# Side matmuls in the last key tiles of an attention loop, and a PSUM bank that returns to the scores three half tiles later

## The chip, the core and the metric

The kernel runs on one NeuronCore of a Trainium2 chip. The core has a matrix engine (TensorE, "PE" in the profile, with its weight loads as "PEld"), VectorE ("DVE"), ScalarE ("ACT"), GpSimd ("POOL") and SyncE ("SP", which here issues the DMAs). Each engine takes its instructions in order and waits for the others by semaphores. Matrix products go to PSUM, eight banks of 128 x 512 float32; VectorE and ScalarE empty them. The metric is the device time of one execution in microseconds (us).

## What is computed

One transformer block with adaptive layer norm on 2048 tokens of width 512: multi-query attention with 32 heads of 16 (one key and value head), then a bilinear gated feed-forward network of inner width 1792.

```python
mod = (silu(c) @ w_mod).reshape(1, 6, 1, 512)      # sa, ca, ga, sb, cb, gb
h = layernorm(x) * (1 + ca) + sa
q, k, v = h @ wq (32 heads), h @ wk, h @ wv        # k, v: 2048 x 16
p = softmax(q k^T / 4);  o = p v
x = x + ga * (o @ wo)
h = layernorm(x) * (1 + cb) + sb
x = x + gb * (((h @ w_gate) * (h @ w_up)) @ w_down)
```

All products whose precision matters are made from two float16 halves of each operand, as three terms (high x high, low x high, high x low). One 128 x 512 result over 512 inputs takes 4 x 3 = 12 matmuls, and one of the down projection, over 1792 inputs, takes 14 x 3 = 42.

## The kernel before

**Units and steps.** The attention runs in 32 units (`NU`): 4 blocks of 512 queries, and in each block 8 groups of 4 heads. A unit goes over 16 key tiles of 128 keys (`KT`), each in two half tiles, so it has 32 steps (`NSTEP`) and the loop has 1024. In a step stand, in this order: half of the row-maximum work (`max_half(0)`: a score matmul into a bank "mx" at L507 and a max reduction on VectorE at L509), two score matmuls with their exps on ScalarE (`qk_exp`, L549 and L551), and the other half of the maximum work. The maximum work is 40 steps (`LEAD`) ahead of the rest, so the last 40 steps of the loop have none. On odd steps follow the four products P times V of the key tile before (`pv`, L558, two passes each). On even steps side work may follow.

**Banks.** Scores use two banks "sc" in turn, and every third score the bank "spare", if `spare["scores"]` is set. Maxima use three banks "mx"; "pv" and "misc" are one bank each. A score matmul waits until the exp of the last score in its bank is done.

**Side work.** While the loop is in block b, PE also does the rest of block b-1: the output projection `wo_work` (4 groups of 12 matmuls), four transposes with the second layer norm (`ln2_work`), gate and up (28 groups of 12) and down (4 groups of 42). Groups are taken by two, as a `duo`: each matmul is cut into two of 64 rows, one of each group, that run side by side on the two halves of the array. One such couple is a "pair". A duo of groups of n matmuls has two turns of n pairs; in the second the halves are swapped. It holds the banks "misc" and "spare". When it ends, its first group is emptied at once (`g0.post`) and the second (`g1.post`) two steps later, from `late`. While a duo runs, or one waits whose gate is open, or `spare["held"]` is over zero, the scores keep to their two banks.

**The planner.** The queue `fill` is filled at step 16 of a block's first unit (L1120 to L1128). Each entry has a step by which it is due. On every even step `pace` works out how many pairs must go per even step so that all are done in time, and adds this to `credit` (9 at most); for the last batch, with its due step past 992, `RESERVE / PAIR` pairs are left out of the count and so kept for the tail. `fill_gap` then issues a burst of at most 6 pairs (`BURST`): it divides what is left of the turn by the credit, rounds that to a number of bursts, and issues one of them. A burst ends with its turn. A duo begins only if `open_gate` allows it and, in the last 16 steps (`2 * LAST_TILES`), not at all.

**The tail.** After the loop come the last P times V and `pv_out` (L564 to L572: ScalarE copies the sums out, SyncE writes them and the row sums to their places). What `fill` still holds becomes `tail`, in plain form: full-height matmuls (L465). The last normalisation goes through DMAs: row sums are read back (`rc`, L579), inverted on VectorE (L582, L583), written, and read spread over partitions (`rr`, L587), then multiplied and split (L591 to L595). `cover(budget)` issues matmuls of `tail`, counted at 216 ns, between these steps, so that PE has work while they run. Then `wo_work(3)`, `ln2_work(3)`, the rest of `tail`, and `ffn_work(3)` follow; nothing of attention is left to run beside them. The last step of a down group is L746 on VectorE and an output DMA on SyncE (L748); that of a wo group is L640, and that of an up group L731.

Of the kernel before, what the change touches and what calls it, by code (L numbers as in the profile page):

```python
# [21 lines left out]
NB = 4  # L22
BT = S // NB
UB = H // 4
NU = NB * UB
# [8 lines left out]
FILL0 = 18  # L34
QPRE = 20
QPRE0 = 26
RESERVE = 35000.0
NRM_GAP = 2
BN_GAP = 1
LN_GAP = 2  # L40
# [2 lines left out]
BURST = 6  # L43
NHF = 10
V_STEP = 34
DUE = 12
QDUE = 40
LAST_TILES = 8
PAIR = 218.0


# [1 line left out]
def adaln_mqa_glu_kernel(ctx: ExitStack, tc: tile.TileContext, x_in, wq_in, wk_in, wv_in, wo_in,  # L53
# [384 lines left out]
    def half(p, g, i, r, start, stop):  # L438
        left, right = g.op(i)
        nc.tensor.matmul(p, left[64 * r:64 * r + 64], right[64 * r:64 * r + 64], start=start, stop=stop)  # L440

    def duo(g0, g1, tags=("misc", "spare")):

        ps = g0.pre(tag=tags[0]), g1.pre(tag=tags[1])
        n = g0.n
        for turn in range(2):
            for i in range(n):
                for r in range(2):
                    half(ps[r ^ turn], (g0, g1)[r ^ turn], i, r, turn == 0 and i == 0, turn == 1 and i == n - 1)
                if turn == 0 or i < n - 1:  # L450
                    yield i == n - 1
        g0.post(ps[0])

        def late():
            spare["held"] -= 1
            g1.post(ps[1])

        spare["held"] += 1
        after(2, late)
# [84 lines left out]
    def qk_exp(u, kt, p, a):  # L544
        s = sst[u % 3]
        if (u, kt, p) not in ptl:
            ptl[u, kt, p] = work.tile([128, 2, D], F32, name="P", tag="P", bufs=4)
        t = ps_sc()
        nc.tensor.matmul(t, kst[64 * a:64 * a + 50, kt * 128:(kt + 1) * 128],  # L549
                         s[64 * a:64 * a + 50, p, :], start=True, stop=True)  # L550
        nc.scalar.activation(ptl[u, kt, p][:, a, :], t, AF.Exp)  # L551

    def pv(u, kt):
        if kt == 0:
            pvb[u] = psum.tile([128, 512], F32, name="pv", tag="pv", bufs=1)
        for j in range(4):
            p, a = divmod(j, 2)
            nc.tensor.matmul(pvb[u][32 * j:32 * j + 32, :], vst[:, kt, :], ptl[u, kt, p][:, a, :],  # L558
                             start=(kt == 0), stop=(kt == KT - 1))

    def pv_out(u):
        b, g = divmod(u, UB)
        ev = work.tile([128, BT], F32, name="ev", tag="ev", bufs=3)
        nc.scalar.activation(ev, pvb[u], AF.Copy)  # L564
        if g % 2 == 0:
            oc[b, g // 2] = work.tile([128, BT], F32, name="oc", tag="oc", bufs=2)
            rsum[b, g // 2] = dram.tile([8, BT], F32, name=f"rs{b}_{g // 2}")
        h = 4 * (g % 2)
        for j in range(4):
            r = 16 * (h + j)  # L570
            nc.sync.dma_start(oc[b, g // 2][r:r + 16, :], ev[32 * j:32 * j + 16, :])
        nc.sync.dma_start(rsum[b, g // 2][h:h + 4, :], ev[16:128:32, :])  # L572
# [30 lines left out]
    def after(delay, f):  # L603
        if tick[0] is None:
            f()
        else:
            timers.setdefault(tick[0] + delay, []).append(f)
# [329 lines left out]
    NSTEP = 32  # L937
# [3 lines left out]
    def drain_posts():  # L941
        todo = posts[:]
        posts.clear()
        if tick[0] is not None:
            tick[0] += 1
            todo += timers.pop(tick[0], [])
        for f in todo:
            f()

    def max_half(a):  # L950
        u, i = divmod(mstep[0], NSTEP)
        if a == 1:
            mstep[0] += 1
        if u >= NU:
            return
        max_mm(u, i, a)
        if a == 1 and u + 1 < NU and i == (QPRE if u else QPRE0):
            load_q(u + 1)
        if i == NSTEP - 1 and a == 1:
            max_fin(u)  # L960
            (_, f, g), = max_rows(u)
            later[mstep[0] + 2] = (f, g)
# [9 lines left out]
    fill = deque()  # L972
    cur = {"gen": None, "left": 0, "swapped": -9}
    credit = [0.0]

    def pace(step):
# [4 lines left out]
        for _, kind, what, due in fill:  # L981
            n += 4.0 if kind == "solo" else 2 * what[0].n
            kept = RESERVE / PAIR if due > (NB * UB - 1) * NSTEP else 0.0
            most = max(most, (n - kept) / max((due - step) / 2, 1.0))
        return most

    def open_gate(step):
        if not fill:
            return False
        gate = fill[0][0]  # L990
        if gate[0] is None:
            gate[0] = step + gate[1]
        return gate[0] <= step

    def fill_gap(step):


        if cur["gen"] is None:
            if not open_gate(step):
                return  # L1000
            _, kind, what, due = fill.popleft()
            if kind == "solo":
                _, f, post = what
                credit[0] -= 4.0
                f()
                if post:
                    posts.append(post)
                return
            if NU * NSTEP - step < 2 * LAST_TILES:
                fill.appendleft(([0, 0], kind, what, due))  # L1010
                return
            begin(step, what, due)
        parts = max(1, round(cur["turn"] / max(credit[0], 1.0)))
        burst(step, min(-(-cur["turn"] // parts), BURST))

    def begin(step, two, due, tags=("misc", "spare")):
        cur.update(gen=duo(*two, tags=tags), left=2 * two[0].n, turn=two[0].n, second=False, due=due, swapped=-9)

    def burst(step, n):
        for _ in range(n):  # L1020
            swap = next(cur["gen"], None)
            credit[0] -= 1.0
            cur["left"] -= 1
            cur["turn"] -= 1
            if swap is None:
                cur["gen"], cur["left"] = None, 0
                return
            if swap:
                cur["turn"], cur["second"], cur["swapped"] = cur["left"], True, step
                return  # L1030
# [57 lines left out]
    for u in range(NU):  # L1088
        b, g = divmod(u, UB)
        if u == 1:  # L1090
            side.extend(dlist)
        for i in range(NSTEP):
            step = u * NSTEP + i
            kt, p = divmod(i, 2)
            drain_posts()
            spare["scores"] = not spare["held"] and cur["gen"] is None and not (fill and fill[0][1] == "duo" and open_gate(step))
            max_half(0)
            qk_exp(u, kt, p, 1)
            qk_exp(u, kt, p, 0)
            max_half(1)  # L1100
            if p == 1:
                if kt == 0:
                    if u > 0:
                        pv(u - 1, KT - 1)
                        posts.append(lambda u=u: pv_out(u - 1))
                else:
                    pv(u, kt - 1)
                late_max()
            elif fill or cur["gen"]:
                credit[0] = min(credit[0] + pace(step), 9.0)  # L1110
                if credit[0] >= 1.0:
                    fill_gap(step)
            side_step(step)
            if u > 0 and g % 2 == 0 and i in (4, 8, 14):
                if i == 4:
                    nrm = normalise((u - 1) // UB, ((u - 1) % UB) // 2)
                nrm[(4, 8, 14).index(i)]()
            if i == 16 and u > 0 and g == 0:
                ln = ln2_work(b - 1)
                due = (b + 1) * UB * NSTEP + (DUE if b < NB - 1 else -8)  # L1120
                gate = [step + 4, 0]
                for two in twos(wo_work(b - 1)):
                    fill.append((gate, "duo", two, due))
                for gap, it in zip((TR_GAP, LN_GAP, LN_GAP, LN_GAP), ln):
                    fill.append(([None, gap], "solo", it, due))
                gate = [None, FFN_GAP]
                for two in ffn_twos(b - 1):
                    fill.append((gate, "duo", two, due))  # L1128
# [7 lines left out]

    u = NU - 1

    if cur["gen"] is not None:
        assert cur["second"]  # L1140
        for _ in cur["gen"]:
            pass
    pv(u, KT - 1)
    pv_out(u)
    ring["tags"] = [("misc", 1), ("spare", 1)] + [("mx", NMX)] * NMX + [("sc", NSC)] * NSC
    tail = deque(plain(g) for _, _, two, _ in fill for g in two)

    def cover(budget):
        while tail and budget > 0:
            drain_posts()  # L1150
            if next(tail[0], None) is None:
                tail.popleft()
            budget -= 216
        drain_posts()
# [3 lines left out]
            for _ in plain(g):  # L1158
                pass

    cover(6000)
    nrm = normalise(NB - 1, KC - 1)
    nrm[0]()
    cover(3000)
# [31 lines left out]
```

## Time and profile before

| | us |
|---|---|
| runs (3): median, lowest, highest | 1826.44, 1825.76, 1830.4 |
| profiled execution, its own time | 1827.18 |
| span of that execution, first to last instruction | 1825.4 |
| first tail matmul behind the last P times V | 1661.82 |
| busy in the span: PE, VectorE, ScalarE, GpSimd | 1714.7, 1438.3, 1217.3, 488.7 |

Times in the rows of a profile count from the start of the span. A row of the timeline has the start, the duration of the merged instructions, the engine, the line, the operation, output and inputs, and the number of instructions; in brackets stands how long the engine was idle before it and what ended this. A matmul of 64 rows is recorded by itself, so a pair is two records; one P times V has two records for each of its four matmuls. "Granted clock" is the share of its full clock that TensorE had.

### The profile page before, as it was taken

How to read it: one execution, taken by the hardware profiler on the slowest of the kernel's cores; microseconds unless marked ns; L12 is line 12 of the kernel's file. 1: busy time of each engine (PE TensorE's matmuls, PEld its weight loads, DVE VectorE, ACT ScalarE, POOL GpSimd, SP SyncE). 2: the span in 40 equal slices, each digit the busy share in tenths (PEclk: the TensorE clock that was granted, in tenths of full speed). 3: DMA queues.
4: the chain of work that ended last, by engine and by line, in shares of the span. 5: the costliest groups of instructions: out<-in, count | busy, mean ns of one | idle time of the engine just before them, and what ended most of it. 6: DMA issues, size and time to landing. Idle time of an engine off the chain costs nothing.

```text
span 1825.4 us, 32237 instructions
## 1 busy us (share of the span) xinstructions
PE 1714.7 (94%) x12643; PEld 554.1 (30%) x12643; DVE 1438.3 (79%) x2441; ACT 1217.3 (67%) x2269; POOL 488.7 (27%) x688
## 2 busy tenths in 40 slices
PE   6899999889989999999999999999989999998999
PEld 3332222222223333333223333333223323322444
DVE  7877999999998888888998888888989888911210
ACT  4567788777777767776677767676777777772110
POOL 5834453436566811010021010100011010111130
PEclk9999999999999999999999999999999999998999
DMA  5212222112221200000100000000100000001000
GB/s 189 91 69 94 60 69 61 49 44 65 82 70 55 55 15 9 5 14 17 50 9 15 9 15 9 6 14 20 46 8 15 9 15 9 11 4 39 18 1 23
DMA packets 49795, 66.58 MB, mean 36 GB/s; under 512 B 16166, under 2 KB 30314, under 8 KB 49644
## 3 DMA queue, kind: packets, MB, share of 16 engines
q1 hardware_dynamic: 48060, 64.33, 11.4%
q8 instruction: 99, 1.62, 0.4%
q14 instruction: 52, 0.43, 0.1%
q10 hardware_dynamic: 1584, 0.20, 0.1%
HBM read 51.12 MB, written 8.92 MB: 33 GB/s over the span
## 4 chain that ended last, share of the span: by engine, by line
PE 68%; DVE 17%; ACT 10%; issue 2%; DMA 2%; POOL 1%; SPq 0%; DVEq 0%; POOLq 0%; ACTq 0%
PE pv L558 22%; PE misc L440 17%; DVE mpart L509 13%; PE mx L507 10%; PE sc L549 10%; PE misc L465 8%; ACT P L551 8%; DVE gf L731 1%; DMA xbig<-in_A_x_dram 1%; ACT ev L564 1%; DVE x L640 0%; DVE x L746 0%; ACT qf L476 0%; DVE oc L591 0%; ACT q L475 0%
## 5 line engine op out<-in xcount | busy, mean ns | idle before, releaser
L509 DVE TENSOR_REDUCE mpart<-mx 128x1 f32<-128x512 f32 x2048 | 1294.2, 684 | 172.3 <-PE sc L549 136.3
L551 ACT ACTIVATE P<-sc 128x512 f32<-128x512 f32 x2048 | 1097.7, 599 | 391.6 <-PE sc L549 385.0
L549 PE MATMUL sc<-sst,kst 50*128 50x512 f16 x2048 | 630.5, 382 | 52.7 <-ACT P L551 35.3
L507 PE MATMUL mx<-kst,sst 48*128 48x512 f16 x2048 | 656.3, 383 | 22.8 <-DVE mpart L509 19.6
L558 PE MATMUL pv<-P,vst 128*32 128x512 f32 x4096 | 552.2, 612 | 0.0
L507 PEld LDWEIGHTS <-sst 48*128 48x128 f16 x2048 | 161.8, 94 | 602.7 <-issue 545.7
L732 POOL TENSOR_SCALAR glu<-gf 128x512 f16<-128x512 f32 x56 | 34.6, 618 | 556.0 <-DVE gf L731 555.9
L549 PEld LDWEIGHTS <-kst 50*128 50x128 f16 x2048 | 136.5, 94 | 107.0 <-issue 66.8
L440 PE MATMUL misc<-h2T,wg 64*128 64x512 f16 x1008 | 134.6, 375 | 7.7 <-DVE gf L731 7.7
L558 PEld LDWEIGHTS pv<-P,vst 128*32 128x32 f32 x4096 | 81.1, 108 | 186.4 <-issue 181.7
L440 PE MATMUL misc<-h2T,wu 64*128 64x512 f16 x1008 | 132.6, 375 | 0.4 <-ACT g L725 0.4
L731 DVE TENSOR_TENSOR gf<-misc,g 128x512 f32<-128x512 f32 x56 | 38.3, 686 | 102.4 <-PE misc L465 62.9
L594 POOL TENSOR_SCALAR och<-oc 128x512 f16<-128x512 f32 x15 | 9.3, 618 | 305.4 <-DVE oc L591 165.9
L440 PE MATMUL misc<-wd,glu 64*128 64x512 f16 x672 | 85.6, 375 | 1.9 <-DVE x L746 1.1
L725 ACT ACTIVATE g<-misc 128x512 f32<-128x512 f32 x56 | 34.0, 608 | 78.7 <-PE misc L465 75.5
L465 PE MATMUL misc<-wd,glu 128*128 128x512 f16 x336 | 74.0, 382 | 0.0
L440 PEld LDWEIGHTS <-wg 64*128 64x128 f16 x1008 | 50.7, 94 | 71.8 <-issue 19.4
L440 PEld LDWEIGHTS <-wu 64*128 64x128 f16 x1008 | 50.3, 94 | 60.2 <-issue 8.8
L733 POOL TENSOR_TENSOR glu<-gf,glu 128x512 f16<-128x512 f32 x56 | 64.7, 1155 | 4.7
L440 PE MATMUL misc<-h,wq 64*128 64x512 f16 x384 | 52.9, 391 | 1.6 <-ACT qf L476 1.6
L815 POOL TENSOR_TENSOR wsl<-wsl 128x448 f32<-128x448 f32 (+1 forms) x40 | 39.0, 975 | 55.9 <-DMA wsl<-in_B_w_up_dram 30.3
L817 POOL TENSOR_TENSOR kwb<-kwb,wsl 128x448 f32<-128x448 f32 (+1 forms) x40 | 47.6, 1189 | 3.1
(214 smaller groups left out, 912.8 us busy)
## 6 DMA issues: line engine op xcount, KB each, us to landing
wsl<-in_B_w_gate_dram SPq DMA_DIRECT2D x32, 224.0 KB
wsl<-in_B_w_up_dram SPq DMA_DIRECT2D x32, 224.0 KB
wsl<-in_B_w_down_dram SPq DMA_DIRECT2D x28, 256.0 KB
sst<-qd SPq DMA_DIRECT2D x186, 32.0 KB
qd<-q SPq DMA_DIRECT2D x16, 256.0 KB
oc<-ev SPq DMA_DIRECT2D x128, 32.0 KB
rr<-ri SPq DMA_DIRECT2D x16, 256.0 KB
xl<-in_A_x_dram SPq DMA_DIRECT2D x16, 256.0 KB
```

The costliest lines, as they stand in the source:

```text
L440: nc.tensor.matmul(p, left[64 * r:64 * r + 64], right[64 * r:64 * r + 64], start=start, stop=stop)
L465: nc.tensor.matmul(p, left, right, start=i == 0, stop=i == g.n - 1)
L507: nc.tensor.matmul(m, s[64 * a:64 * a + 48, p, t * 128:(t + 1) * 128], kst[64 * a:64 * a + 48, kc * 512:(kc + 1) * 512], start=True, stop= ...
L509: nc.vector.tensor_reduce(mparts[u][:, a, p, t, kc:kc + 1], m, axis=AX.X, op=OP.max)
L549: nc.tensor.matmul(t, kst[64 * a:64 * a + 50, kt * 128:(kt + 1) * 128], s[64 * a:64 * a + 50, p, :], start=True, stop=True)
L551: nc.scalar.activation(ptl[u, kt, p][:, a, :], t, AF.Exp)
L558: nc.tensor.matmul(pvb[u][32 * j:32 * j + 32, :], vst[:, kt, :], ptl[u, kt, p][:, a, :], start=(kt == 0), stop=(kt == KT - 1))
L731: nc.vector.tensor_tensor(gf, p, st["g", f], op=OP.mult)
L732: nc.gpsimd.tensor_scalar(st["glu"][:, 0, f, :], gf, 1.0, 0.0, op0=OP.mult, op1=OP.add)
L733: nc.gpsimd.tensor_tensor(st["glu"][:, 1, f, :], gf, st["glu"][:, 0, f, :], op=OP.subtract)
L815: nc.gpsimd.tensor_tensor(acc if i == 0 else t, t, t, op=OP.mult)
L817: nc.gpsimd.tensor_tensor(acc, acc, t, op=OP.add)
```

## The change

Four things are edited. `late` still empties the second bank two steps after the duo, but the count that keeps the scores off that bank is lowered three steps later, by `free`. The rule of the last 16 steps is gone; instead `open_gate` refuses a duo of groups of n matmuls when fewer than 2 * ceil(n/6) + 2 steps are left: 6 for n = 12, 16 for n = 42. In a first turn `fill_gap` takes at least as many pairs as are needed to end that turn two steps before the loop does. A duo that is still in its second turn when the loop ends is finished behind the last P times V and `pv_out`, and its pairs (216 ns each) count towards the first `cover`. For the last batch the reserve falls from 35000 to 31000 ns and the due step moves from 1016 to 1020.

```diff
-RESERVE = 35000.0
+RESERVE = 31000.0
...
-LAST_TILES = 8
+LAST_DUE = -4
...
         def late():
+            g1.post(ps[1])
+            after(3, free)
+
+        def free():
             spare["held"] -= 1
-            g1.post(ps[1])
...
     def open_gate(step):
         if not fill:
             return False
+        if fill[0][1] == "duo" and NU * NSTEP - step < 2 * -(-fill[0][2][0].n // BURST) + 2:
+            return False
...
-            if NU * NSTEP - step < 2 * LAST_TILES:
-                fill.appendleft(([0, 0], kind, what, due))
-                return
             begin(step, what, due)
         parts = max(1, round(cur["turn"] / max(credit[0], 1.0)))
-        burst(step, min(-(-cur["turn"] // parts), BURST))
+        n = min(-(-cur["turn"] // parts), BURST)
+        if not cur["second"]:
+            n = max(n, -(-cur["turn"] // max((NU * NSTEP - 2 - step) // 2, 1)))
+        burst(step, n)
...
-                due = (b + 1) * UB * NSTEP + (DUE if b < NB - 1 else -8)
+                due = (b + 1) * UB * NSTEP + (DUE if b < NB - 1 else LAST_DUE)
...
-    if cur["gen"] is not None:
-        assert cur["second"]
-        for _ in cur["gen"]:
-            pass
     pv(u, KT - 1)
     pv_out(u)
+    left = cur["left"]
+    if cur["gen"] is not None:
+        assert cur["second"] and NU * NSTEP - cur["swapped"] > 2
+        for _ in cur["gen"]:
+            drain_posts()
...
-    cover(6000)
+    cover(6000 - 216 * left)
```

## The prediction, made before the changed kernel was timed

> **What bounds the kernel now.** I read the page first, for the engines and the groups of instructions.
>
> ```profile
> span 1825.4 us, 32237 instructions
> PE 1714.7 (94%) x12643; PEld 554.1 (30%) x12643; DVE 1438.3 (79%) x2441; ACT 1217.3 (67%) x2269; POOL 488.7 (27%) x688
> L465 PE MATMUL misc<-wd,glu 128*128 128x512 f16 x336 | 74.0, 382 | 0.0
> ```
>
> TensorE bounds most of the span, but not evenly, so the place matters. The last row tells what stands behind the loop: 336 full-height matmuls of the down projection are 8 groups of 42, four of the last block and four of block 2. So the whole down projection of block 2 (168 matmuls) is left for the tail. Next I read the windows of 5 us around the end of the loop. Columns: stretch, its length, busy time (and instructions) of PE, PEld, DVE, ACT, POOL, then granted clock, DMA share, GB/s.
>
> ```profile
> 1635.00:1640.00 5.00, 4.82 (x36) 1.38 (x36) 0.88 (x2) 4.02 (x8) 0.10 (x1) 1.00 0.01 3
> 1640.00:1645.00 5.00, 3.41 (x23) 0.56 (x16) 0.41 (x1) 3.59 (x8) 3.42 (x4) 1.00 0.00 0
> ...
> 1655.00:1660.00 5.00, 4.32 (x24) 0.67 (x20) 0.00 (x0) 2.17 (x4) 0.00 (x0) 0.50 0.00 0
> ```
>
> From 1640 no engine is full, and by 1655 the granted clock is 0.50. The timeline of that stretch shows why nothing is full. It has one key tile (two steps of the loop) per block; L549 are the scores, L440 side pairs, L558 P times V.
>
> ```profile
> 1637.72 0.39 PE L549 MATMUL sc<-sst,kst 50*128 50x512 f16 x2
> ...
> 1637.95 1.03 PE L440 MATMUL misc<-h2T,wu 64*128 64x512 f16 x8
> ...
> 1640.58 0.39 PE L549 MATMUL sc<-sst,kst 50*128 50x512 f16 x2
> ...
> 1641.66 0.86 PE L549 MATMUL sc<-sst,kst 50*128 50x512 f16 x2 [0.68 <-ACT P L551]
> ...
> 1643.44 0.39 PE L549 MATMUL sc<-sst,kst 50*128 50x512 f16 x2
> ```
>
> A key tile with four side pairs (1637.72 to 1640.58) takes 2.86 us, and one with none (1640.58 to 1643.44) also 2.86. The scores have two banks, and the second pair of scores waits for the exp that empties them (0.68 us). Side pairs fit into that wait for nothing. After 1639 there are none, because the old kernel begins no side duo in the last 16 steps; six key tiles run with the gap open, and then at a reduced clock.
>
> **The change part by part.** A step is half a key tile; 1024 steps, side bursts on even ones.
>
> *How many pairs move.* At step 784 the planner queues 2 wo duos of 24 pairs, 14 gate/up duos of 24, 2 down duos of 84, and 4 transposes counted as 4: 568 units. Before it keeps back 35000/218 = 160.6 and aims at step 1016: 407.4 over 115 even steps from 786, or 3.54 a burst. The 400 units ahead of the down duos then end with the 113th burst, step 1010. The trace agrees: its last burst of four pairs is at 1637.95. After, it keeps 31000/218 = 142.2 and aims at 1020: 425.8/117 = 3.64, so the 400 are done with the 110th burst, at step 1004. At 1006 a down duo may open (18 steps left, 2*7+2 = 16 needed). Its first turn of 42 pairs must run in 7 bursts of 6 (1006 to 1018), and the second turn puts 6 into 1020 and 1022. That makes **54 pairs in the loop**, 30 behind the last P times V, and 84 matmuls in the tail in place of 168.
>
> *The tail.* A pair of half-height matmuls or one full one costs the PE the same:
>
> ```profile
> 1600.14 1.46 PE L440 MATMUL misc<-h2T,wu 64*128 64x512 f16 x12
> ```
> ```profile
> 1696.70 124.77 PE misc L465 x578
> ```
>
> 124.77/578 = 0.216 us a matmul; the 12 halves are six pairs, 1.46 us with the last one's drain. The tail is one stream of matmuls, so 54 fewer are 54 x 0.216 = **-11.7 us**. What the removal could uncover is the last normalisation, for which this work is the cover. PE, DVE and SyncE there:
>
> ```profile
> 1658.25 3.64 PE L558 MATMUL pv<-P,vst 128*32 128x512 f32 x16
> 1661.82 15.24 PE L465 MATMUL misc<-wd,glu 128*128 128x512 f16 x66
> ...
> 1679.81 0.39 PE L465 MATMUL misc<-wo,och 128*128 128x512 f16 x1 [0.80 <-DVE och L594]
> 1680.53 8.38 PE L465 MATMUL misc<-wo,och 128*128 128x512 f16 x38 [0.34 <-DVE och L595]
> ```
> ```profile
> 1671.92 0.75 DVE L746 SCALAR_TENSOR_TENSOR x<-misc,sca,x 128x512 f32<-128x512 f32 x1 [31.51 <-PE misc L465]
> 1672.59 0.23 DVE L582 TENSOR_SCALAR rc<-rc,kb 128x32 f32<-128x32 f32 x1
> ```
> ```profile
> 1665.66 0.53 SPq L572 DMA_DIRECT2D rs<-ev  x1
> 1667.36 0.32 SPq L579 DMA_DIRECT2D rc<-rs  x1
> ```
>
> Before, 66 matmuls cover it and PE still waits 0.80 + 0.34 us. After, 30 pairs and 38 matmuls cover it, 68, nearly the same. On the chain, two things move. The reciprocal (L582) stood behind L746, which waited for the first down group (42 matmuls); now both L746 of the duo come after 30 pairs, about 1661.8 + 6.6, and end by +8.2. But the duo's first output DMA is now issued ahead of the rc read on SP, so that read goes from +5.5 to about +7.9, lands an estimated 1.5 to 2 us later (the rs write, issued by 1666.2, let rc go 1.2 us on), and L582 starts near +9.7 instead of +10.8. PE comes to wo sooner too, since its clock stays up. I take -0.3 us; bounds are -1.1 (the wait gone) and +2.1 (no gain on the DVE side and the read's 2.4 us all on the chain). Behind wo, 28 matmuls stay ahead of the transposes as before, and 18 (3.9 us) behind them instead of 74; the last h2T half is needed only 9 matmuls further on, so that still holds.
>
> *The clock.* Two P times V take 3.64 us at that reduced clock. A key tile with six pairs, behind the max work, at full clock:
>
> ```profile
> 1599.91 0.39 PE L549 MATMUL sc<-sst,kst 50*128 50x512 f16 x2
> ...
> 1601.77 1.06 PE L558 MATMUL pv<-P,vst 128*32 128x512 f32 x8
> ...
> 1602.81 0.55 PE L549 MATMUL sc<-sst,kst 50*128 50x512 f16 x2
> ```
>
> Its P times V, from 1601.77 to the next score, takes 1.04, so two are 2.0 to 2.1: **-1.6 us**. The 66 matmuls take 15.24 where 66 x 0.216 and 0.17 of drain are 14.4: **-0.8 us**. [...]
>
> *The last nine key tiles, with six pairs each.* Before:
>
> ```profile
> 1631.01 1.07 PE L558 MATMUL pv<-P,vst 128*32 128x512 f32 x8
> ...
> 1651.03 1.06 PE L558 MATMUL pv<-P,vst 128*32 128x512 f32 x8
> ...
> 1654.10 1.93 PE L558 MATMUL pv<-P,vst 128*32 128x512 f32 x8
> ```
>
> From 1631.01 to the last block's start at 1658.25 they take 27.2 us. The tile of six pairs above takes 2.90 (1599.91 to 1602.81). Nine are 26.1; I add 0.2 because the first must wait for the last up group's VectorE product in the spare bank: 26.3, **-1.0 us**. The dear end is six pairs beside the max work:
>
> ```profile
> 1556.87 1.06 PE L558 MATMUL pv<-P,vst 128*32 128x512 f32 x8
> 1560.13 1.07 PE L558 MATMUL pv<-P,vst 128*32 128x512 f32 x8
> 1563.05 1.07 PE L558 MATMUL pv<-P,vst 128*32 128x512 f32 x8
> ```
>
> The first interval holds six pairs and is 3.26, the second three and is 2.92. Nine at 3.26 would be 29.3, +2.1. I take the tile without max work, since none runs in the last 40 steps.
>
> *Steps 786 to 1004.* Followed burst by burst, the faster pace changes little: 15 bursts of six before and after, 4 of five against 5, but two of the sixes come earlier, beside the max work, where six cost 0.34 more than three (3.26 and 2.92): +0.7. The stretch without it has two fewer; I take 0.2 for each, between 0.34 and the nothing of 2.90 against 2.86: -0.4. **+0.3 us.**
>
> *The spare bank.* Only where no further duo waits do scores take the bank back: six times, at steps 40, 296, 524, 552, 780 and 814. There the score matmul stands before the evacuation:
>
> ```profile
>   DVE x L640: 3.9, 3
>   ACT qf L476: 1.9, 2
>   DVE x L746: 1.3, 2
> ```
> ```profile
> 926.32 0.39 PE L507 MATMUL mx<-kst,sst 48*128 48x512 f16 x1
> 928.48 0.39 PE L549 MATMUL sc<-sst,kst 50*128 50x512 f16 x2 [1.77 <-DVE x L640]
> ...
> 930.41 1.93 PE L558 MATMUL pv<-P,vst 128*32 128x512 f32 x8
> ```
> ```profile
> 174.30 1.06 PE L558 MATMUL pv<-P,vst 128*32 128x512 f32 x8
> ...
> 176.78 1.06 PE L558 MATMUL pv<-P,vst 128*32 128x512 f32 x8
> ```
>
> At best all of it goes: -7.1 us. At worst nothing goes, and three half tiles each run at two banks' 2.86 a key tile instead of three banks' 2.48 (174.30 to 176.78): 18 x 0.19 = +3.4. Most of the wait is not the bound, though: VectorE works through it without a break, on the same evacuation and the max reductions, and stands idle only behind it:
>
> ```profile
> 932.92 1.29 DVE L509 TENSOR_REDUCE mpart<-mx 128x1 f32<-128x512 f32 x2 [1.25 <-PE sc L549]
> ```
> ```profile
> 1345.47 1.89 DVE L509 TENSOR_REDUCE mpart<-mx 128x1 f32<-128x512 f32 x3 [0.51 <-PE sc L549]
> ```
>
> I count these two idle times as won, 1.8 us, and give back 0.8: 0.57 (3 x 0.19) at step 40, where no VectorE evacuation hides the two banks, and 0.2 for the five others. **-1.0 us.**
>
> *Sum.* -11.7 - 1.6 - 0.8 - 0.3 - 1.0 + 0.3 - 1.0 = -16.1. The profiled execution took 1827.18 us (its span 1825.4 and 1.8 around it): 1811.1. It stands 0.7 above the runs' median 1826.44. I say **1811**.
>
> **The rivals.**
> 1. *The clock still falls.* [...] Then the 1.6 and 0.8 stay, and 1.5 of the last two key tiles (1651.03 to 1654.10 and to 1658.25: 3.07 and 4.15 us in place of 2.86): 1811 + 3.9 = 1815. For it: a short stop (the wait of 1.77 us is followed by a P times V of 1.93). Against it: with side pairs the clock reads 1.00 to 1640. 12%.
> 2. *The normalisation is uncovered*, because the output DMA goes ahead of the rc read: +2.4, and with six pairs a tile at the dear price (+2.1 in place of -1.0) another 3.1: 1813 to 1817. The rows of SP speak for the first, the timeline at 1599.91 against the second. 12%.
> 3. *The stalls at the spare bank were all real*: -7.1 instead of -1.0, 1805. VectorE's unbroken row speaks against it. 8%.
> 4. *It does not do what it says*: the gate/up pairs end one burst or two later than I count; from step 1010 the down duo stays shut, and the last tiles run empty as now, 1826. The margin is one even step (1008 would still open). 4%.
> 5. *Slower.* Scores held to two banks behind every duo and not behind six: 56 duos end in the loop, at 0.57 us each 31.9, so 1811 + 1.0 + 31.9 = 1844. It decides from 27 ends on (15.1/0.57). Against it: between duos of one queue the scores are shut out already, and the key tiles there show no third bank. 3%.
>
> The forecast itself has 61%.
>
> **How the numbers follow.** The range joins the forecast with its neighbours: below, the spare bank's -7.1 (1805); above, the clock rival with some of the second (1815 to 1819): 1804 to 1819. Outside lie rivals 4 and 5 and the tails, under 2 in 10. A measurement of this kernel tells about 0.3% (5.5 us) from no change: faster needs less than 1821. Forecast, rivals 1 to 3 and a little doubt: faster 0.91, same 0.06, slower 0.03.
>
> **What would show it.** In the windows: PE near 4.8 of 5 and clock 1.00 from 1635 to the tail. In the groups: L465 misc<-wd,glu x252 instead of x336, and L440 misc<-wd,glu x840 instead of x672. In the timeline: twelve L440 rows in each of the last nine key tiles at 2.9 us. In the waits: no PE sc L549 <- DVE x L640. If key tiles of six pairs take 3.27 there, or wo waits over 2 us for och, or the clock drops all the same, the term of that name was wrong.

## The result and the profile after

The changed kernel takes 1812.04 us (median of 6 runs, 1807.56 to 1813.56) where the kernel before takes 1826.10 (6 runs). The ratio is 0.9916, with a 95% interval of 0.9904 to 0.9928: 14 us, or 0.8%, less. The forecast was 1811. The profiled execution took 1810.53 us, with a span of 1808.8, which is 16.6 below the span before.

First the groups of instructions of the changed kernel (lines have moved by three; L440 is the side pair, L468 the full-height matmul):

```profile
span 1808.8 us, 32406 instructions
PE 1706.7 (94%) x12727; PEld 557.4 (31%) x12727; DVE 1434.5 (79%) x2441; ACT 1218.1 (67%) x2269; POOL 490.5 (27%) x688
L440 PE MATMUL misc<-wd,glu 64*128 64x512 f16 x840 | 106.4, 375 | 1.9 <-DVE x L749 1.1
L468 PE MATMUL misc<-wd,glu 128*128 128x512 f16 x252 | 55.1, 379 | 0.0
```

One down duo has gone from full height (336 to 252) to pairs (672 to 840 halves), as counted. Next the windows at the end of the loop; the columns are those of the windows shown before.

```profile
1640.00:1645.00 5.00, 5.00 (x48) 2.89 (x48) 0.00 (x0) 3.45 (x8) 0.00 (x0) 1.00 0.00 0
...
1655.00:1660.00 5.00, 5.00 (x44) 2.17 (x42) 0.00 (x0) 2.77 (x5) 0.00 (x0) 1.00 0.00 0
1660.00:1665.00 5.00, 5.00 (x48) 2.24 (x46) 0.00 (x0) 0.00 (x0) 0.00 (x0) 1.00 0.13 31
```

PE is busy in all of them, and the granted clock stays at 1.00, where it was 0.50 from 1655 before. PE's timeline from the ninth last key tile on:

```profile
1630.05 1.07 PE L561 MATMUL pv<-P,vst 128*32 128x512 f32 x8
...
1653.69 1.07 PE L561 MATMUL pv<-P,vst 128*32 128x512 f32 x8
1654.69 0.50 PE L552 MATMUL sc<-sst,kst 50*128 50x512 f16 x2
1654.91 1.57 PE L440 MATMUL misc<-wd,glu 64*128 64x512 f16 x12
1656.21 0.50 PE L552 MATMUL sc<-sst,kst 50*128 50x512 f16 x2
1656.63 2.18 PE L561 MATMUL pv<-P,vst 128*32 128x512 f32 x16
1658.75 6.65 PE L440 MATMUL misc<-wd,glu 64*128 64x512 f16 x60
1665.33 8.38 PE L468 MATMUL misc<-wd,glu 128*128 128x512 f16 x38
1673.54 10.84 PE L468 MATMUL misc<-wo,och 128*128 128x512 f16 x48
```

Six pairs (12 records) stand in the key tile, which takes 2.94 us (1653.69 to 1656.63); nine of them take 26.6 (1630.05 to 1656.63) where the nine before took 27.2 with 12 pairs in all. The two last P times V take 2.18 instead of 3.64. Behind them come 30 pairs, then 38 matmuls, and the 48 of wo run through: of the waits of 0.80 and 0.34 us for `och`, 0.14 us is left in this execution. On the chain that they cover:

```profile
1665.44 1.41 DVE L749 SCALAR_TENSOR_TENSOR x<-misc,sca,x 128x512 f32<-128x512 f32 x2 [34.14 <-PE misc L440]
1668.47 0.24 DVE L585 TENSOR_SCALAR rc<-rc,kb 128x32 f32<-128x32 f32 x1 [1.63 <-DMA rc<-rs]
```
```profile
1666.22 0.34 SPq L751 DMA_DIRECT2D out_dram<-x  x1
1666.67 0.37 SPq L582 DMA_DIRECT2D rc<-rs  x1
```

The output DMA does go ahead of the read of the row sums, and VectorE now waits for that read (1.63 us). It still starts 9.7 us behind the last P times V (1668.47 - 1658.75), not 10.8.

Last, what the scores waited for, with the total in us and the number of times:

```profile
  ACT P L554: 31.4, 115
  ACT qf L479: 0.6, 1
```

The waits for L640 and L746 (5.2 us in five) have gone.

Where the 16.6 us went, by stretches. Each number is the difference of the starts of the P times V rows just ahead of two steps (spans up to the first and from the last):

| stretch (steps) | before | after | |
|---|---|---|---|
| up to 38 | 167.53 | 168.51 | +1.0 |
| 38 to 50, bank returns at 40 | 16.65 | 19.63 | +3.0 |
| 50 to 294 | 331.72 | 330.24 | -1.5 |
| 294 to 304, returns at 296 | 16.35 | 15.84 | -0.5 |
| 550 to 562, returns at 552 | 20.31 | 18.59 | -1.7 |
| 776 to 788, returns at 780 | 17.70 | 17.15 | -0.6 |
| 788 to 1006 | 332.41 | 331.75 | -0.7 |
| 1006 to the last but one P times V | 27.24 | 26.58 | -0.7 |
| from there to the end | 167.15 | 152.17 | -15.0 |

The stretches between that are left out agree to 0.03 us. No bank returns in the rows "up to 38" and "50 to 294"; over the thirteen profiles of this case they scatter from 165.7 to 170.8 and from 328.7 to 332.0, so their +1.0 and -1.5 are not put down to the change.

### The profile page after: what moved, and what is told of

It reads as the page before. It is cut to its first block, busy times and chain, and to the rows that moved or that the text cites. A ratio compares the mean times of both kernels' runs of the same rounds, so it can differ in the third digit from the quotient of the medians.

```text
span 1808.8 us, 32406 instructions
## 1 busy us (share of the span) xinstructions
PE 1706.7 (94%) x12727; PEld 557.4 (31%) x12727; DVE 1434.5 (79%) x2441; ACT 1218.1 (67%) x2269; POOL 490.5 (27%) x688
## 4 chain that ended last, share of the span: by engine, by line
PE 69%; DVE 15%; ACT 11%; issue 2%; DMA 2%; POOL 1%; SPq 0%; DVEq 0%; ACTq 0%; POOLq 0%
PE pv L561 22%; PE misc L440 18%; DVE mpart L512 12%; PE mx L510 10%; PE sc L552 10%; ACT P L554 8%; PE misc L468 7%; DVE gf L734 1%; ACT ev L567 1%; DMA xbig<-in_A_x_dram 1%; DVE x L643 0%; DMA wsl<-in_B_w_gate_dram 0%; DVE mh L522 0%; ACT qf L479 0%; ACT q L478 0%
## 5 line engine op out<-in xcount | busy, mean ns | idle before, releaser
L440 PE MATMUL misc<-h2T,wg 64*128 64x512 f16 x1008 | 133.9, 375 | 7.7 <-DVE gf L734 7.7
L440 PE MATMUL misc<-h2T,wu 64*128 64x512 f16 x1008 | 132.3, 375 | 0.5 <-ACT g L728 0.5
L440 PE MATMUL misc<-wd,glu 64*128 64x512 f16 x840 | 106.4, 375 | 1.9 <-DVE x L749 1.1
L440 PEld LDWEIGHTS <-wg 64*128 64x128 f16 x1008 | 50.5, 94 | 71.4 <-issue 18.3
L440 PEld LDWEIGHTS <-wu 64*128 64x128 f16 x1008 | 50.1, 94 | 60.4 <-issue 8.2
L440 PEld LDWEIGHTS <-glu 64*128 64x128 f16 x840 | 46.1, 94 | 46.5 <-issue 5.7
L468 PE MATMUL misc<-wd,glu 128*128 128x512 f16 x252 | 55.1, 379 | 0.0
L440 PE MATMUL misc<-h,wq 64*128 64x512 f16 x384 | 53.0, 392 | 1.6 <-ACT qf L479 1.6
```

The costliest lines, as they stand in the source:

```text
L468: nc.tensor.matmul(p, left, right, start=i == 0, stop=i == g.n - 1)
```

## The experiments

**The two parts apart.** First the later return alone, in the kernel before; then the rest without it.

```diff
         def late():
-            spare["held"] -= 1
             g1.post(ps[1])
+            after(3, free)
+
+        def free():
+            spare["held"] -= 1
```

> The kernel before with the later return of the second bank alone. Theory (the wait at the spare bank counts only where VectorE idles behind it): 1 us less than before, within 0.3% of it; in the profile the waits of scores for L640 and L746 are gone, the key tiles at steps 552, 780 and 814 are shorter by 0.5 to 1.7 us each and those at step 40 longer by 1 to 3. Rival (the stalls were all real): 6 to 7 us less. Rival (two banks cost the whole difference, nothing is won): 3.4 us more.

Measured: 1828.68 us, ratio 1.0004 (0.9992 to 1.0017). By itself the later return gives nothing that can be measured. In its profile the return at 552 takes 18.58 us for 550 to 562 (20.31 before), and the one at 780 17.16 (17.70), as expected; 38 to 50 takes 18.59 instead of 16.65. 810 to 838, around the return at 814, takes 44.41 instead of 43.60, which is against the expectation; the granted clock is 0.50 there from 1341.1 to 1348.0. The interval (1.5 us less to 3.1 more) leaves out the rival of 6 to 7 us less and, just, that of 3.4 more. The theory's 1 us less lies inside it.

The changed kernel with the old `late`:

```diff
         def late():
-            g1.post(ps[1])
-            after(3, free)
-
-        def free():
             spare["held"] -= 1
+            g1.post(ps[1])
```

> The changed kernel with the second bank returned at once, as before. Theory: it keeps 15.1 of the 16.1 us, so about 15 us less than the kernel before (ratio 0.992), with 54 pairs fewer behind the loop and the clock at 1.00 there. If the later return carried the gain instead, it would stay within 3 us of the kernel before.

Measured: 1812.99 us, ratio 0.9924 (0.9912 to 0.9937). The work at the end of the loop carries the gain. The changed kernel lies 0.8 thousandths lower (0.9916), within the intervals of both.

**The clock without the pairs.** The kernel before, with unread matmuls where the last key tiles are empty:

```diff
             if NU * NSTEP - step < 2 * LAST_TILES:
                 fill.appendleft(([0, 0], kind, what, due))
+                if "ps" not in junk:
+                    junk["ps"] = ps_misc(tag="misc"), ps_misc(tag="spare")
+                for i in range(6):
+                    for r in range(2):
+                        half(junk["ps"][r], what[r], i, r, True, True)
                 return
```

> The kernel before, with six pairs of matmuls whose result nobody reads in each of the six key tiles that have no side work (steps 1012 to 1022); the down projection stays in the tail as it was. So the gaps are filled and no work moves. Theory (the gaps make the clock fall): the granted clock stays at 1.00 from 1640 to 1665, the two last P times V take 2.1 us, the first 66 matmuls of the tail 14.4, and the time is 3 to 4 us less than before. Rival (only longer idle times lower the clock, so it falls anyway): clock 0.5 as before and no time won, or up to 1 us lost by the longer key tiles.

Measured: 1823.96 us, ratio 0.9987 (0.9977 to 0.9997): 0.5 to 4 us less, though the kernel does 72 matmuls more. Its windows, and PE's timeline:

```profile
1645.00:1650.00 5.00, 5.00 (x42) 1.90 (x41) 0.00 (x0) 3.65 (x7) 0.00 (x0) 1.00 0.00 0
...
1655.00:1660.00 5.00, 5.00 (x40) 1.94 (x37) 0.00 (x0) 2.97 (x6) 0.00 (x0) 1.00 0.00 0
```
```profile
1657.07 2.15 PE L558 MATMUL pv<-P,vst 128*32 128x512 f32 x16
1659.15 14.42 PE L465 MATMUL misc<-wd,glu 128*128 128x512 f16 x66
```

The clock stays at 1.00, the two P times V take 2.15 us and the first 66 matmuls 14.42 (15.24 before). So the clock fell because of the gaps, and it can be had without moving any work. From step 1012 to the end this profile is 3.4 us shorter than the one before: +0.3 from 1012 to 1020, -1.3 from 1020 to 1024 and -2.4 behind.

**The change without the moved pairs.** One constant of the changed kernel:

```diff
-RESERVE = 31000.0
+RESERVE = 32000.0
```

> The changed kernel with the reserve at 32000 ns instead of 31000. By the planner's arithmetic the gate and up pairs then end too late for a down duo to open, so no pair moves: 168 matmuls in the tail. The shut gate also gives the scores their third bank in the last eight key tiles. Theory: the 11.7 us of the moved pairs are gone; the clock still falls; the third bank shortens those tiles from 2.86 to about 2.5 us, some 3 us; with the spare bank's 1 us that is 4 us less than the kernel before, 12 us more than the changed one. If it were the rest of the change that paid and not the moved pairs, it would stay within 3 us of the changed kernel.

Measured: 1823.19 us, ratio 0.9985 (0.9971 to 0.9999). Without the pairs most of the gain is gone. One point came out otherwise than expected: the clock does not fall. PE's timeline has scores in three banks there (three at once, then one):

```profile
1650.43 0.60 PE L552 MATMUL sc<-sst,kst 50*128 50x512 f16 x3
1651.50 0.37 PE L552 MATMUL sc<-sst,kst 50*128 50x512 f16 x1 [0.47 <-ACT P L554]
1651.80 1.07 PE L561 MATMUL pv<-P,vst 128*32 128x512 f32 x8
...
1654.18 1.06 PE L561 MATMUL pv<-P,vst 128*32 128x512 f32 x8
```
```profile
1650.00:1655.00 5.00, 4.06 (x32) 0.72 (x24) 0.00 (x0) 4.38 (x10) 0.00 (x0) 1.00 0.00 0
```

A key tile with no side work takes 2.38 us instead of 2.86, PE is busy 4.06 of 5 us, and the clock is 1.00. So the third bank alone also shortens the end of the loop, in part.

**More pairs in the loop.** The same constant the other way, to 25000:

> The changed kernel with the reserve at 25000 ns. By the planner's arithmetic the whole first down duo, 30 pairs more, is then done in the loop and 84 matmuls are left for the tail, of which 66 go ahead of the last output projection, 18 behind it and none behind the transposes. Theory (gaps in the loop are full by now, and the tail needs its cover): the pairs bring nothing there (0.2 us a pair in the loop against 0.216 in the tail), and PE waits 3 to 5 us around the transposes of the tail: 2 to 5 us more than the changed kernel. Rival (every moved pair goes on paying): 6.5 us less.

Measured: 1812.41 us, ratio 0.993 (0.9915 to 0.9944), against 0.9916 for the changed kernel: 30 pairs more in the loop bring nothing, and may cost some. PE's timeline of the tail:

```profile
1677.29 2.11 PE L468 MATMUL misc<-wo,och 128*128 128x512 f16 x9
1680.42 0.39 PE L468 MATMUL misc<-wo,och 128*128 128x512 f16 x1 [1.03 <-DVE och L597]
1681.15 8.38 PE L468 MATMUL misc<-wo,och 128*128 128x512 f16 x38 [0.34 <-DVE och L598]
1689.36 4.05 PE L468 MATMUL misc<-wd,glu 128*128 128x512 f16 x18
1693.25 0.49 PE L686 MATMUL misc<-ident,n 128*128 128x128 f32 x3
1694.82 1.64 PE L686 MATMUL misc<-ident,n 128*128 128x128 f32 x13 [1.08 <-ACT n L661]
1696.48 4.29 PE L468 MATMUL misc<-h2T,wg 128*128 128x512 f16 x12
1700.61 2.75 PE L468 MATMUL misc<-h2T,wu 128*128 128x512 f16 x12
```

The missing cover shows in three places. The 48 matmuls of wo take 1.4 us more than in the changed kernel (waits of 1.03 and 0.34), the transposes 1.5 more (a wait of 1.08), and the first gate group behind them 1.5 more (1696.48 to 1700.61 is 4.13, against 2.59). Together 4.4 us, so the part behind the loop is 2.1 us shorter and not 6.5. In the loop, 838 to 984 takes 4.1 us more (226.6 against 222.5).

**The return at step 40.** This was the one that lost in the profile after. Windows around it, of the kernel before and then of the changed one:

```profile
170.00:175.00 5.00, 3.71 (x28) 0.89 (x25) 3.29 (x6) 5.00 (x11) 3.48 (x4) 1.00 0.30 91
175.00:180.00 5.00, 4.64 (x36) 1.11 (x32) 5.00 (x9) 4.31 (x9) 4.84 (x6) 1.00 0.44 143
```
```profile
170.00:175.00 5.00, 3.81 (x28) 1.03 (x25) 4.44 (x7) 5.00 (x10) 2.50 (x3) 1.00 0.13 48
175.00:180.00 5.00, 4.89 (x23) 0.90 (x26) 2.71 (x6) 3.22 (x7) 4.84 (x6) 0.61 0.55 173
180.00:185.00 5.00, 5.00 (x30) 1.00 (x23) 3.36 (x6) 2.82 (x6) 4.78 (x5) 0.71 0.53 152
```

PE is as busy in the first window, but in the second the clock is 0.61 and the three key tiles from step 40 take 4.35, 3.87 and 3.55 us where they took 3.86, 2.48 and 2.46. Two kernels ask why. In the first, four unread matmuls fill the wait:

```diff
+            elif spare["held"] and cur["gen"] is None and u == 1:
+                j = ps_misc(tag="misc")
+                for i in range(4):
+                    nc.tensor.matmul(j, wq[:, 0, i, 0:128], h16[:, 0, i, 0:BT], start=True, stop=True)
             elif fill or cur["gen"]:
```

> The changed kernel with four unread matmuls into the free bank misc at steps 40 and 42 each, where the scores wait for exps and no side work is there. Theory (part of the loss at step 40 is the clock, lowered by the PE's wait of 1.05 us): the granted clock stays at 1.00 from 170 to 190 us, the key tiles at 42 and 44 take 2.9 and 2.5 us instead of 3.9 and 3.6, and the stretch 38 to 50 takes some 17.8 us instead of 19.6. Rival (two banks alone make it long): 19.6 us or more, the matmuls coming on top.

Measured: 1810.78 us, ratio 0.9917 (0.9902 to 0.9933). The place is as the theory has it:

```profile
170.00:175.00 5.00, 4.87 (x36) 1.57 (x32) 4.19 (x7) 4.55 (x10) 1.94 (x2) 1.00 0.12 46
175.00:180.00 5.00, 4.89 (x34) 1.13 (x32) 3.42 (x7) 3.81 (x9) 4.84 (x6) 1.00 0.61 201
```

Clock 1.00, 38 to 50 in 17.71 us, the tiles at 42 and 44 in 3.04 and 2.47. This is one execution, but without the unread matmuls a P times V at this place took 1.93 us, where its neighbours take 1.06, in the changed kernel (at 179.65), in its second profile below (177.32) and with the reserve at 25000 (178.82). The whole time does not show it beyond its interval. In the second kernel the bank returns at once there:

```diff
         def late():
             g1.post(ps[1])
-            after(3, free)
+            if tick[0] < 100:
+                free()
+            else:
+                after(3, free)
```

> The changed kernel, but the bank returns at once behind the query projections (steps 10 to 40), where ScalarE empties it, and three half tiles later only behind duos that VectorE empties. Theory: the key tiles at steps 38 to 50 go from 19.6 back to 16.7 to 17.8 us, the others stay as in the changed kernel: 1 to 3 us less than the changed kernel, ratio about 0.990 to the kernel before. Rival (the return makes no difference anywhere): the same as the changed kernel within 1 us.

Measured: 1808.17 us, ratio 0.9904 (0.9888 to 0.9919). Its profile has 18.04 us for 38 to 50, because the clock is 0.66 from 175 to 180 here as well: an early return does not keep it up either. (The profile of the run above that keeps the old `late` has 17.83 for 38 to 50. In the second profile of the early return, below, a P times V at 175.61 takes 1.93 us; but with the return at once the clock is 1.00 from 175 to 180 in the kernel before and in the last run of this section.) The stretch 294 to 304, whose instructions were not touched, takes 17.92 us instead of 15.84, also at a lowered clock (1.00 from 518 to 533 in the changed kernel):

```profile
520.00:525.00 5.00, 3.82 (x22) 0.69 (x20) 5.00 (x10) 2.21 (x5) 2.68 (x10) 0.84 0.44 138
525.00:530.00 5.00, 5.00 (x22) 0.96 (x19) 3.08 (x7) 3.08 (x6) 4.17 (x12) 0.50 0.28 76
```

So at the same stop the clock fell in one execution and not in the other. The kernel was run again, beside the changed kernel itself:

> The changed kernel with the bank returned at once behind the query projections, a second time, beside the changed kernel itself on one chip. Theory: 1 to 3 us less than the changed kernel. Rival: no difference beyond 1 us.

> The changed kernel itself, for comparison on one chip: 14 to 16 us less than the kernel before.

Measured: 1807.72 us and a ratio of 0.9891 (0.9876 to 0.9906), beside 1812.09 us and 0.9914 (0.9900 to 0.9928) for the changed kernel. Twice the early return behind the query projections comes out lower than the changed kernel, by 1.2 and 2.3 thousandths; the intervals still overlap. Its median is the lowest of the kernels tried.

**Two that did not give what was expected.** That kernel with three unread matmuls behind every duo that no other follows:

```diff
+            if p == 0 and cur["gen"] is None and tick[0] < warm[0]:
+                j = ps_misc(tag="misc")
+                for _ in range(3):
+                    nc.tensor.matmul(j, kst[:, 0:128], kst[:, 0:512], start=True, stop=True)
```

> The changed kernel with the bank returned at once behind the query projections, and three unread matmuls into the free bank misc on the two even steps behind every duo that no other follows. Theory (a short stop of the PE at such a place lowers the clock in some executions and not in others): the granted clock stays at 1.00 at all six places; the stretches 38 to 50, 294 to 304 and 810 to 838 take 16.7, 15.8 and 41.4 us; 2 to 4 us less than the changed kernel, and less than the kernel with the early return alone by about 2. Rival (the clock does not hang on these stops): no less than the early return alone.

Measured: 1810.88 us, ratio 0.9905 (0.9891 to 0.9920), not less than the early return alone. 294 to 304 and 810 to 838 came out as expected (15.96 and 41.54 us), but not step 40: the key tile there takes 5.66 us, and the clock is 0.66 from 175 to 180 all the same.

And the later return behind VectorE's duos alone, in the kernel before:

```diff
         def late():
-            spare["held"] -= 1
             g1.post(ps[1])
+            if tick[0] < 100:
+                free()
+            else:
+                after(3, free)
```

> The kernel before with the later return alone, but only behind duos that VectorE empties; behind the query projections the bank returns at once, as before. Theory (five returns win, the one at step 40 loses): the stretches at 294, 550 and 776 are shorter by some 2.8 us together, the one at 38 is as before: 2 to 4 us less than the kernel before, where the later return at all six places gave nothing. Rival (the later return does nothing): within 1 us of the kernel before.

Measured: 1825.72 us, ratio 0.9990 (0.9979 to 1.0001), which does not decide between the two. 38 to 50 takes 16.65 as before, 550 to 562 is 1.7 us shorter and 776 to 788 0.5, but 294 to 304 takes 17.70 instead of 16.35 and 810 to 838 44.45 instead of 43.60.

## Why the prediction was right, by its steps

*The moved pairs, -11.7.* Right. Behind the last but one P times V the changed kernel takes 152.17 us and the kernel with unread pairs 164.73, both with the clock at 1.00 in the windows shown. Of these 12.6 us, 0.9 is the wait for `och` (0.70 and 0.34 with the unread pairs, 0.14 in the changed kernel), and 11.7 is the pairs. With the reserve at 32000, where no pair moves, this gain is gone.

*The clock, -1.6 and -0.8.* Right, in the profile (the two P times V go from 3.64 to 2.18) and by the kernel that fills the gaps and moves nothing (2.15, and 14.42 for the 66 matmuls). The rival by which the clock falls in any case is out.

*The last nine key tiles, -1.0.* They gave 0.7. The first took 3.03 us (its wait was 0.1, not 0.2) and the others 2.94, not 2.90. The dear price of 3.26 did not come, as argued: no max work runs there.

*The wait for wo, -0.3.* Mis-sized: 0.14 us is left of 1.14, so -1.0 in this profile. VectorE started at +9.7 as worked out, but the chain from there to the last half of `och` was 0.4 us shorter than before, and with 68 matmuls for 66 that was nearly enough. The size varies from one execution to the next: in the seven profiles with this tail, PE idles 0.14 to 0.74 us there.

*Steps 786 to 1004, +0.3.* Right in size. 788 to 1006 gave -0.7, but -1.1 of it lies in 810 to 838, around the return at 814, where both profiles have a lowered clock, of different length (0.50 for twice 3.41 us before, once after). The rest is 0.5 longer.

*The spare bank, -1.0.* By itself it measures between 1.5 us less and 3.1 more. Half of the reasoning held: where VectorE worked on through the wait nothing was won (522 to 532: 14.11 and 14.10). Two steps failed. The first is the pair of idle times counted as won. In the profile before, both fall into a stretch at half clock: the one ends at 932.92 and the clock is 0.50 from 929.66 to 933.07, the other ends at 1345.47 and the clock is 0.50 from 1342.67 to 1346.08. The kernel that fills the gaps at the end of the loop has the old return too, and its profile keeps the clock at 1.00 at the first place (from 925.47 to 932.29). Its PE and VectorE there, at 552:

```profile
929.48 0.39 PE L549 MATMUL sc<-sst,kst 50*128 50x512 f16 x2 [1.76 <-DVE x L640]
```
```profile
932.63 6.96 DVE L509 TENSOR_REDUCE mpart<-mx 128x1 f32<-128x512 f32 x11
```

The scores wait as long as before, but VectorE does not stand idle, and 550 to 562 takes 19.02 us. So of the 1.7 us there 1.3 is the clock of that one execution, and 0.4 (19.02 to 18.59) is the return. At 814 VectorE has no idle time either. At 780, where the prediction expected no gain, 0.5 us is won (17.70 to 17.16). The second is the term "0.57 at step 40": in the profiles it is 1.9 to 3.0 us. Two banks cost 0.5 us in the first key tile (3.86 to 4.35) and at most 0.6 in the next (3.04 against 2.47, with unread matmuls in it); the lowered clock costs the rest, which the kernel with four unread matmuls takes away.

*Luck in the total.* -16.1 was forecast and the two profiles differ by 16.6, but the terms do not agree as closely. The end of the loop and the tail gave 15.7 where 15.4 was summed. The parts before them came to -0.9, near the -0.7 summed, only because +3.0 at step 40 and +1.0 ahead of it stand against -1.5 of scatter and losses of clock in the profile before. The medians differ by 14.1 us.

*What stays open.* Which of the six places loses its clock in a given execution; the last section shows one part of the answer. Profiles of single executions differ there by 1 to 3 us for the same instructions, more than the return of the bank is worth.

## What to carry to other kernels

When a kernel saves work to cover a latency at its end, look at the last stretch of the loop before it: here key tiles with no side work took as long as those with four pairs (2.86 us), so the work could run there for nothing, until the tiles were full; beyond that, moving more brought nothing (30 pairs more: 1812.41 us against 1812.04). A stretch where PE is partly idle can cost twice, in the gaps and then at a lowered clock (here 2.4 us behind the loop and 1.3 in its last two key tiles), and filling the gaps with useless matmuls is a quick way to measure the second cost by itself. Before a wait is removed, look whether the engine that ends it works on without a break: then there is little to win (here 14.11 and 14.10 us). If that engine does stand idle, look at the clock there first: one profile at a lowered clock shows idle time that the wait did not make (here VectorE's 1.25 us at 552, which is not there at 1.00).

## What the runs showed of the hardware

The granted clock fell although PE was never idle for long: at the end of the loop before, the gaps were 0.68 us, with PE busy 3.41 of 5 us. With PE busy 4.06 of 5 (reserve 32000) it did not fall; around the bank's returns it fell in some executions and not in others: with 3.71 from 170 to 175 it stayed at 1.00 in the kernel before, and with 3.71 (bank returned at once) and 3.81 (changed kernel) it was 0.66 and 0.61 in the next 5 us. Nor does the longest gap decide it, as the wait at 552 shows (1.77 and 1.76 us). These are windows cut where the clock changes, in the kernel before and then in the one with unread pairs, whose code is the same at 552:

```profile
926.25:929.66 3.41, 1.27 (x10) 0.32 (x7) 3.33 (x7) 0.44 (x2) 1.38 (x6) 1.00 0.00 0
929.66:933.07 3.41, 3.20 (x14) 0.58 (x15) 2.17 (x6) 1.75 (x5) 1.63 (x7) 0.50 0.01 2
...
1653.28:1663.52 10.24, 9.51 (x35) 1.62 (x34) 0.00 (x0) 4.21 (x8) 0.00 (x0) 0.50 0.01 2
```
```profile
925.47:928.88 3.41, 2.24 (x17) 0.54 (x14) 3.38 (x8) 1.57 (x3) 0.01 (x1) 1.00 0.09 22
928.88:932.29 3.41, 2.22 (x17) 0.56 (x18) 3.33 (x6) 2.06 (x4) 1.94 (x8) 1.00 0.01 2
```

In the profiles before and after the clock is at 1.00 or at 0.50 and at nothing between. A lowered stretch lasts 3.41 us, twice that (6.83, after, from 176.09) or three times (10.24, before, from 1653.28), but for the last of each, which goes on past the last instruction. In each of the two profiles all changes of the clock lie on one grid of 3.41 us (before, 933.07 to 1342.67 is 120 of them; after, 418.44 to 1340.04 is 270), and the two grids lie 0.77 us apart, counted from the start of the span. In the windows above, one window of the grid before holds the whole wait (PE busy 1.27 of 3.41 us), and the clock falls at its end; with unread pairs the wait is shared by two windows (2.24 and 2.22), and it does not.

Between 110 and 1680 us these two profiles have ten falls, seven before and three after. Each came at the end of a window of the grid in which PE was busy for 37 to 70% of the time; none of the 898 windows busier than 71% was followed by one. But ten windows of 71% or less were not followed by a fall either, the emptiest with PE busy 2.12 of 3.41 us (before, from 1288.06). So in these two profiles every fall had a low busy share in the window before it, and such a share was not enough; what else is needed stays open.
